# Raw loads of the first three head pairs over two hardware DMA queues, values first in the other queue, early relus on two engines, the last store in two

## The chip, the cores and the metric

The kernel runs on one core of a Trainium2 chip. The core has a matrix engine (TensorE; PE in the profile, its weight loads PEld), VectorE (DVE), ScalarE (ACT), GpSimd (POOL) and SyncE (SP), which here only issues DMAs. Data moves between device memory and the core's on-chip memory by DMA, on 16 DMA engines that all queues share. POOL feeds one queue (software_dynamic in the profile, q0), in which a transfer may also cast; SP and ScalarE feed hardware queues (hardware_dynamic, q1), which copy as is. The metric is the device time in microseconds (us).

## What is computed

Attention with one added to the softmax's denominator, and then a feed-forward layer with a squared relu:

```python
# q, k, v: (8 batches, 12 heads, 448 positions, 64), fp32
scores = scale * q @ k^T                      # scale = 1/8
e = exp(scores - m)                           # m: row maximum
attn = e / (sum(e) + exp(-m) + 1e-9)          # exp(-m) is the added one
x = (attn @ v).transpose(0, 2, 1, 3).reshape(3584, 768)
h = x @ w_in                                  # 768 -> 2048
g = relu(h) ** 2
out = g @ w_out                               # 2048 -> 768, fp32
```

The kernel takes no maximum: it computes `exp(scores)` and divides by `sum + 1`, which is the same.

## The kernel before

**Tiling.** Heads are taken in pairs, two heads of 64 on the 128 partitions, so that a batch has six pairs. A unit of attention is a pair of one batch: `scores` (q k^T into PSUM, L163), `exp` on ScalarE (L153), `add_chunks` on VectorE (sums over the key chunks, L194), `row_sums` (a matmul with ones, then logarithm and negated exponential on ScalarE, that is, a reciprocal, L225), `values` (L218) and `normalise` on VectorE into the tile `xt` (L237). Batch 0 has twelve units: six pairs with 192 queries each, then six with the other 256. The other batches have six units of 448 queries. The order is software-pipelined by hand (L372 to 416): in iteration i, the scores and exponentials of unit i stand with the row sums, values and normalisation of unit i - 1.

**Feed-forward.** `mlp_in` (L247) and `mlp_out` (L272) are generators. When a stretch of tokens is normalised, they are queued, and `drain` puts some of their matmuls between the steps of the attention units, by a share that is set where they are queued. The first stretch has 128 tokens. For it `mlp_in` takes four blocks of 128 hidden columns at a time (`f0` = 0, 4, 8, 12), each followed by a relu on ScalarE (L263) and a square on VectorE (L267). For all other stretches the relu is on VectorE (L265). `mlp_out` copies each block of 128 tokens from PSUM in two pieces of 512 and 256 columns (ScalarE, L283) and then stores the 768 columns in one go (SP, L295).

**Loads and queues.** Weights, values and most of q and k come by POOL's queue and are cast to fp16 on the way. For batches 0 and 1, q and k lie in the on-chip memory as they are read ("natural"); `regroup` on VectorE (L139) puts them in order, PE transposes them (L146), and VectorE copies the result from PSUM (L149). Regrouping stands two units ahead of the scores, transposing one. So the regroup of pair 3 stands on VectorE in iteration 1, ahead of that unit's `add_chunks`. For later batches, q and k go through a staging buffer and a transposing DMA.

In the order in which the loads are issued: q and k of pairs 0 and 1 of batch 0 as fp32 by SP (tiles `qr`, `kr`, L88); by POOL (tiles `qn`, `kn`, L91; `vn`, L79) q and k of pair 2, v of pairs 0 to 2, then, after the identity for the transposes has been made on POOL, q, k and v of pairs 3 to 5, four of eight parts of `win`, and then batch 1 and the rest of the weights. A tile `qn` or `kn` is used again by batch 1, whose load waits for the last regroup from it. Nine matmuls on zeros (L363) run on PE at the start, and more of them between the first units.

The instructions of an engine run in the order of the program. Each tile pool has a fixed number of buffers; the pool of the reciprocal has one for each of its two tiles.

Of the kernel before, what the change touches and what calls it, by code (L numbers as in the profile page):

```python
# [8 lines left out]
FP32 = mybir.dt.float32  # L9
FP16 = mybir.dt.float16  # L10
AF = mybir.ActivationFunctionType
# [4 lines left out]
def kernel(  # L16
# [9 lines left out]
    nc = tc.nc  # L26

    B, H, S, D = q.shape
    NT, DM = out.shape
# [4 lines left out]
    RUN = 4  # L34
    P = S // RUN
    ON_PE = (0, 1)
    COLS = H * S // 2 + 16

    scale = 1.0 / float(D) ** 0.5
# [11 lines left out]
    z_pool = ctx.enter_context(tc.tile_pool(name="z", bufs=1))  # L51
# [6 lines left out]
    m_psum = ctx.enter_context(tc.tile_pool(name="m_psum", bufs=3, space=bass.MemoryType.PSUM))  # L58

    ctx.enter_context(tc.manual_schedule())  # L60
    nc.scalar.preload_act_table_set("natural_log_exp_and_others")

    win = persist.tile([128, DCH, DF], FP16, name="win")
    wout = persist.tile([128, NFFB, DM], FP16, name="wout")
# [10 lines left out]
    def load_v(b, p0, p1):  # L75
        hs = slice(2 * p0, 2 * p1)
        if b not in vns:
            vns[b] = v_pool.tile([P, H, RUN, D], FP16, name="vn")
        nc.gpsimd.dma_start(out=vns[b][:, hs], in_=v_r[b, :, hs])  # L79

    def load_natural(b, p0, p1):

        raw = b == 0 and p1 <= 2
        for n, r in (("q", q_r), ("k", k_r)):
            src = r[b, :, 2 * p0:2 * p1]
            if raw:
                t = nat.tile([P, 2, RUN, D], FP32, name=f"{n}r{p0}")
                nc.sync.dma_start(out=t, in_=src)  # L88
            else:
                t = nat.tile([P, NPAIR, RUN, D], FP16, name=f"{n}n{p0 // 3}")  # L90
                nc.gpsimd.dma_start(out=t[:, 0:2 * (p1 - p0)], in_=src)  # L91
            for pr in range(p0, p1):
                naturals[n, b, pr] = t[:, 2 * (pr - p0):2 * (pr - p0) + 2]
# [115 lines left out]
    def of_head(e, u, h):  # L209

        b, _, _, n = u
        if n < S:
            return e[:, h]
        if b in ON_PE:
            return e.rearrange("p (h x) -> p h x", h=2)[:, h]
        return e.rearrange("p (o h x) -> p h o x", o=2, h=2)[:, h]
# [8 lines left out]
    def row_sums(u, es):  # L225
        n = u[3]
        total = es[:, 0:2 * S] if n == S else es[:, 4 * S - 2 * n:4 * S].rearrange("p (h n) -> p h n", h=2)
        zp = m_psum.tile([128, 512], FP32, name="mp")
        for h in range(2):
            nc.tensor.matmul(zp[64 * h:64 * h + 64, 0:n], ones, of_head(total, u, h), start=True, stop=True)  # L230
        lnz = z_pool.tile([128, S], FP32, name="lnz")
        rcp = z_pool.tile([128, S], FP32, name="rcp")
        nc.scalar.activation(out=lnz[:, 0:n], in_=zp[:, 0:n], func=AF.Ln, bias=one_b)  # L233
        nc.scalar.activation(out=rcp[:, 0:n], in_=lnz[:, 0:n], func=AF.Exp, scale=-1.0)  # L234
        return rcp

    def normalise(u, xp, rcp):  # L237
# [9 lines left out]
    def mlp_in(t0, n):  # L247
        gt = gts[t0] = []
        xt, x0 = xts[t0 // (2 * S)], t0 % (2 * S)
        per = max(1, 512 // n) if n < 384 else 1  # L250
        for f0 in range(0, NFFB, per):
            hp = m_psum.tile([128, 512], FP32, name="mp")
            for j in range(per):
                fb = f0 + j
                for dc in range(DCH):
                    nc.tensor.matmul(hp[:, j * n:(j + 1) * n], win[:, dc, fb * 128:(fb + 1) * 128],  # L256
                                     xt[:, dc, x0:x0 + n], start=(dc == 0), stop=(dc == DCH - 1))
                    if j < per - 1 or dc < DCH - 1:
                        yield n / 2.4
            m = per * n  # L260
            rt = r_pool.tile([128, 512], FP16, name="rt")
            if t0 == 0:
                nc.scalar.activation(out=rt[:, 0:m], in_=hp[:, 0:m], func=AF.Relu)  # L263
            else:
                nc.vector.tensor_scalar(out=rt[:, 0:m], in0=hp[:, 0:m], scalar1=0.0, scalar2=None, op0=ALU.max)  # L265
            g = g_pool.tile([128, 512], FP16, name=f"g{f0}")
            nc.vector.tensor_mul(g[:, 0:m], rt[:, 0:m], rt[:, 0:m])  # L267
            for j in range(per):
                gt.append(g[:, j * n:(j + 1) * n])
            yield n / 2.4  # L270

    def mlp_out(t0, n):  # L272
        gt = gts.pop(t0)
        for ts in range(n // 128):
            ot = osb_pool.tile([128, DM], FP32, name="ot")
            for n0, n1 in ((0, 512), (512, DM)):
                op = m_psum.tile([128, 512], FP32, name="mp")
                for fb in range(NFFB):
                    nc.tensor.matmul(op[:, 0:n1 - n0], gt[fb][:, ts * 128:(ts + 1) * 128], wout[:, fb, n0:n1],  # L279
                                     start=(fb == 0), stop=(fb == NFFB - 1))  # L280
                    if fb < NFFB - 1:
                        yield (n1 - n0) / 2.4
                nc.scalar.activation(out=ot[:, n0:n1], in_=op[:, 0:n1 - n0], func=AF.Copy, scale=OUT_SCALE)  # L283
                if n1 < DM:
                    yield (n1 - n0) / 2.4
            c = t0 + ts * 128
            end = c + 128
            while c < end:
                b = c // S
                step = RUN if b in ON_PE else 2  # L290
                rows = out[b * S:(b + 1) * S, :].rearrange("(p t) m -> t p m", t=step)
                t, p = c % S // (S // step), c % (S // step)
                m = min(S // step - p, end - c)
                o = c + 128 - end
                nc.sync.dma_start(out=rows[t, p:p + m, :], in_=ot[o:o + m, :])  # L295
                c += m
            yield (DM - 512) / 2.4


# [3 lines left out]
    nc.vector.memset(ones, 1.0 / GS)  # L303
    one_b = consts.tile([128, 1], FP32)
    nc.vector.memset(one_b, 1.0 / GS)
    load_natural(0, 0, 1)
    load_natural(0, 1, 2)
    load_natural(0, 2, 3)
    load_v(0, 0, 3)
    ident = consts.tile([128, 128], FP16)  # L310
    make_identity(nc, ident)
# [16 lines left out]
    def queue(part, t0, n):  # L328
        work.append((mlp_in if part == 1 else mlp_out)(t0, n))
        left[0] += (NFFB * DCH * n if part == 1 else n // 128 * NFFB * DM) / 2.4  # L330
# [17 lines left out]
    t0 = 384  # L348
    for b in range(1, B):
        n = 384 if b % 2 == 0 else 512  # L350
# [21 lines left out]
    for i in range(NU + 1):  # L372
# [6 lines left out]
        if u:  # L379
            b, pr = u[0:2]  # L380
# [16 lines left out]
        if prev:  # L397
            rcp = row_sums(prev, pes)
            values(prev, pet, xp, 0)
            values(prev, pet, xp, 1)  # L400
            if i < NPAIR:
                keep_warm(1)
# [44 lines left out]
```

The softmax here doesn't subtract the row's maximum and nothing guards it: scores larger than these inputs give would overflow.

## Time and profile before

| what | value |
|---|---|
| median of four runs | 437.62 us (435.66 to 438.82) |
| the profiled execution | 438.7 us, span 436.9 us |
| PE busy | 426.3 us, 98% of the span |
| ACT busy | 248.4 us, 57% |
| DVE busy | 244.8 us, 56% |
| POOL busy | 33.4 us, 8% |
| mean granted clock of PE | 0.992 |
| POOL's DMA queue | 24608 packets, 22.40 MB |
| hardware DMA queues | 54304 packets, 24.34 MB |

The span goes from the first to the last instruction of one execution; the time of that execution is 1.8 us longer. Busy shares are over the whole span and hide that the start and the end look different from the middle. A line of the profile names the engine, the line of the code, the operation and the tiles; "idle before, releaser" says how long the engine stood idle ahead of an instruction and what ended that. In the chain of work that ended last, each step is followed back to what released it.

### The profile page before, as it was taken

Reading aid. Unit: us, or ns where it says so; the run is one execution under the profiler, and the core shown is the slowest. Engines: PE = TensorE matmul, PEld = TensorE weight load, DVE = VectorE, ACT = ScalarE, POOL = GpSimd, SP = SyncE. Lnnn points to the kernel's source line nnn. Section 1 sums busy time; section 2 is a strip of 40 time slices with the busy share of each in tenths; the row PEclk is TensorE's granted clock in tenths of the full one; section 3 lists DMA queues with packets and bytes.
Section 4 is the critical chain, followed back from the end, with each engine's and each line's share of the span. In section 5 each row is a group of like instructions: output and inputs, shape, how many; then the busy total and the mean of one; then the engine's idle time right before and its main releaser. Section 6 shows DMA issues by size and latency. Waiting matters only on the chain.

```text
span 436.9 us, 7530 instructions
## 1 busy us (share of the span) xinstructions
PE 426.3 (98%) x3147; PEld 231.5 (53%) x3147; DVE 244.8 (56%) x487; ACT 248.4 (57%) x361; POOL 33.4 (8%) x52
## 2 busy tenths in 40 slices
PE   8989899999999999999999999999999999999996
PEld 3556574544455555554456555654455555554464
DVE  3857585358822586348842388248762278428700
ACT  2889767664565756675446755764555655740011
POOL 8441100010000100010000100030000000000000
PEclk9989899999999999999999999999999999999999
DMA  9999999289312894259611698039902200010022
GB/s 173 197 197 203 210 213 191 74 145 194 78 38 75 136 204 77 66 83 214 128 27 54 101 224 123 38 56 208 190 1 74 72 3 1 36 59 14 1 72 72
DMA packets 78946, 47.22 MB, mean 108 GB/s; under 512 B 50624, under 2 KB 74944, under 8 KB 78528
## 3 DMA queue, kind: packets, MB, share of 16 engines
q0 software_dynamic: 24608, 22.40, 32.3%
q1 hardware_dynamic: 54304, 24.34, 24.8%
q8 instruction: 24, 0.39, 0.3%
q14 instruction: 10, 0.08, 0.1%
HBM read 45.71 MB, written 19.32 MB: 149 GB/s over the span
## 4 chain that ended last, share of the span: by engine, by line
PE 92%; ACT 3%; DMA 2%; issue 1%; POOL 1%; DVE 1%; ACTq 0%; POOLq 0%
PE mp L256 34%; PE mp L279 34%; PE sp L186 9%; PE xp L222 8%; PE mp L230 3%; PE sp L174 2%; DMA kn<-in_k_dram 2%; ACT et L154 1%; PE mp L146 1%; ACT lnz L233 1%; ACT rcp L234 0%; POOL qn L91 0%; DVE es L203 0%; POOL vn L79 0%; PE mp L363 0%
## 5 line engine op out<-in xcount | busy, mean ns | idle before, releaser
L154 ACT ACTIVATE et<-sp 112x896 f16<-112x896 f32 (+2 forms) x192 | 166.2, 914 | 115.8 <-PE sp L186 94.2
L256 PE MATMUL mp<-xt,win 128*128 128x512 f16 (+3 forms) x864 | 156.9, 335 | 1.5 <-DVE xt L242 1.5
L279 PE MATMUL mp<-wout,g 128*128 128x512 f16 (+1 forms) x896 | 154.2, 326 | 0.0
L279 PEld LDWEIGHTS <-g 128*128 128x128 f16 x896 | 84.2, 98 | 63.2 <-issue 9.6
L256 PEld LDWEIGHTS <-win 128*128 128x128 f16 x864 | 78.4, 99 | 72.2 <-issue 12.6
L199 DVE TENSOR_TENSOR es<-et 112x896 f16<-112x896 f16 x84 | 51.6, 622 | 104.9 <-ACT et L154 104.8
L265 DVE TENSOR_SCALAR rt<-mp 128x512 f16<-128x512 f32 (+1 forms) x120 | 76.0, 633 | 38.5 <-PE mp L256 35.8
L283 ACT ACTIVATE ot<-mp 128x512 f32<-128x512 f32 (+1 forms) x56 | 27.3, 487 | 64.5 <-PE mp L279 63.7
L267 DVE TENSOR_TENSOR g<-rt 128x512 f16<-128x512 f16 (+1 forms) x124 | 49.5, 399 | 6.9 <-ACT rt L263 2.7
L222 PE MATMUL xp<-et,vn 112*64 112x448 f16 (+2 forms) x432 | 46.0, 335 | 0.0
L186 PE MATMUL sp<-qk 64*112 64x224 f16 x576 | 42.8, 268 | 0.0
L186 PEld LDWEIGHTS <-qk 64*112 64x112 f16 x576 | 26.9, 128 | 25.8 <-issue 25.8
L233 ACT ACTIVATE lnz<-mp,one_b 128x448 f32<-128x448 f32 (+2 forms) x54 | 32.2, 597 | 2.0 <-PE mp L230 1.9
L242 DVE TENSOR_TENSOR xt<-xp,rcp 128x448 f16<-128x448 f32 (+2 forms) x54 | 30.5, 566 | 2.7 <-ACT rcp L234 2.7
L234 ACT ACTIVATE rcp<-lnz 128x448 f32<-128x448 f32 (+2 forms) x54 | 28.9, 535 | 1.7
L222 PEld LDWEIGHTS <-vn 112*64 112x64 f16 x432 | 24.5, 110 | 10.0 <-issue 0.4
L79 POOL DMA_DIRECT2D vn<-in_v_dram x10 | 8.9, 890 | 246.8 <-PE xp L222 233.3
L201 DVE TENSOR_TENSOR es<-es 112x896 f16<-112x896 f16 x42 | 26.2, 623 | 1.0
L230 PE MATMUL mp<-es,ones 112*64 112x448 f16 (+2 forms) x108 | 19.4, 355 | 1.8 <-DVE es L207 1.6
L174 PE MATMUL sp<-qk 64*112 64x192 f16 (+2 forms) x144 | 17.3, 315 | 1.5 <-ACT et L154 1.3
L363 PE MATMUL mp<-warm 128*128 128x512 f16 x31 | 11.6, 479 | 1.2 <-DVE warm L301 1.2
L230 PEld LDWEIGHTS <-ones 112*64 112x64 f16 x108 | 6.4, 106 | 11.2 <-issue 5.0
(32 smaller groups left out, 83.2 us busy)
## 6 DMA issues: line engine op xcount, KB each, us to landing
out_dram<-ot SPq DMA_DIRECT2D x12, 384.0 KB, 2.3
vn<-in_v_dram POOLq DMA_DIRECT2D x6, 672.0 KB, 8.8
stage_q<-in_q_dram POOLq DMA_DIRECT2D x5, 676.0 KB, 11.2
stage_k<-in_k_dram POOLq DMA_DIRECT2D x5, 676.0 KB, 13.8
win<-in_moe_w_in_dram POOLq DMA_DIRECT2D x8, 384.0 KB, 14.7
wout<-in_moe_w_out_dram POOLq DMA_DIRECT2D x4, 768.0 KB, 19.5
out_dram<-ot SPq DMA_DIRECT2D x8, 288.0 KB, 2.6
out_dram<-ot SPq DMA_DIRECT2D x8, 192.0 KB, 2.7
```

The lines of the kernel that those rows point to most:

```text
L154: nc.scalar.activation(out=out_, in_=in_, func=AF.Exp, scale=scale)
L186: nc.tensor.matmul(sp[:, odd, h * (S // 2):(h + 1) * (S // 2)], qk[r, which, kx:kx + 2 * P - 1:2], qk[r, 0, x:x + S // 2], start=True, sto ...
L199: nc.vector.tensor_add(f[:, step], e[:, 2 * step], e[:, 2 * step + 1])
L222: nc.tensor.matmul(xp[64 * h:64 * h + 64, 0:n], vns[b][:, 2 * pr + h, kk, :], of_head(chunk(et, u, c, kk), u, h), start=(kk == 0), stop=(k ...
L230: nc.tensor.matmul(zp[64 * h:64 * h + 64, 0:n], ones, of_head(total, u, h), start=True, stop=True)
L233: nc.scalar.activation(out=lnz[:, 0:n], in_=zp[:, 0:n], func=AF.Ln, bias=one_b)
L234: nc.scalar.activation(out=rcp[:, 0:n], in_=lnz[:, 0:n], func=AF.Exp, scale=-1.0)
L242: nc.vector.tensor_mul(xts[b // 2][:, pr, c:c + n], xp[:, 0:n], rcp[:, 0:n])
L256: nc.tensor.matmul(hp[:, j * n:(j + 1) * n], win[:, dc, fb * 128:(fb + 1) * 128], xt[:, dc, x0:x0 + n], start=(dc == 0), stop=(dc == DCH - 1))
L265: nc.vector.tensor_scalar(out=rt[:, 0:m], in0=hp[:, 0:m], scalar1=0.0, scalar2=None, op0=ALU.max)
L267: nc.vector.tensor_mul(g[:, 0:m], rt[:, 0:m], rt[:, 0:m])
L279: nc.tensor.matmul(op[:, 0:n1 - n0], gt[fb][:, ts * 128:(ts + 1) * 128], wout[:, fb, n0:n1], start=(fb == 0), stop=(fb == NFFB - 1))
```

## The change

Five edits, all in one step:

1. q and k of pair 2 of batch 0 are loaded as fp32 into tiles of their own, like pairs 0 and 1. The q loads of the three pairs are issued by SP, the k loads by ScalarE, whose preload of the function table now stands behind them.
2. POOL's queue so begins with v of pairs 0 to 2.
3. Of the four relus of the first stretch, those of `f0` = 4 and 12 go to VectorE.
4. The logarithm is written to the tile of the reciprocal, and the tile `lnz` is gone.
5. Storing is a function of its own. For the last 128 tokens the first 512 columns are stored as soon as they are copied, and the other 256 after that.

```diff
-    nc.scalar.preload_act_table_set("natural_log_exp_and_others")
...
-        raw = b == 0 and p1 <= 2
+        raw = b == 0 and p1 <= 3
...
-                nc.sync.dma_start(out=t, in_=src)
+                (nc.sync if n == "q" else nc.scalar).dma_start(out=t, in_=src)
...
-        lnz = z_pool.tile([128, S], FP32, name="lnz")
         rcp = z_pool.tile([128, S], FP32, name="rcp")
-        nc.scalar.activation(out=lnz[:, 0:n], in_=zp[:, 0:n], func=AF.Ln, bias=one_b)
-        nc.scalar.activation(out=rcp[:, 0:n], in_=lnz[:, 0:n], func=AF.Exp, scale=-1.0)
+        nc.scalar.activation(out=rcp[:, 0:n], in_=zp[:, 0:n], func=AF.Ln, bias=one_b)
+        nc.scalar.activation(out=rcp[:, 0:n], in_=rcp[:, 0:n], func=AF.Exp, scale=-1.0)
...
-            if t0 == 0:
+            if t0 == 0 and f0 % 8 == 0:
                 nc.scalar.activation(out=rt[:, 0:m], in_=hp[:, 0:m], func=AF.Relu)
...
+    def store(c, ot, n0, n1):
+        end = c + 128
+        while c < end:
+            b = c // S
+            step = RUN if b in ON_PE else 2
+            rows = out[b * S:(b + 1) * S, n0:n1].rearrange("(p t) m -> t p m", t=step)
+            t, p = c % S // (S // step), c % (S // step)
+            m = min(S // step - p, end - c)
+            o = c + 128 - end
+            nc.sync.dma_start(out=rows[t, p:p + m, :], in_=ot[o:o + m, n0:n1])
+            c += m
...
                 nc.scalar.activation(out=ot[:, n0:n1], in_=op[:, 0:n1 - n0], func=AF.Copy, scale=OUT_SCALE)
+                if n1 == DM or t0 + ts * 128 + 128 == NT:
+                    store(t0 + ts * 128, ot, 0 if n1 < DM or t0 + ts * 128 + 128 < NT else n0, n1)
...
-    load_natural(0, 0, 1)
-    load_natural(0, 1, 2)
-    load_natural(0, 2, 3)
+    for pr in range(3):
+        load_natural(0, pr, pr + 1)
+    nc.scalar.preload_act_table_set("natural_log_exp_and_others")
     load_v(0, 0, 3)
```

More of the change, by code (lines that the diff above doesn't have):

```diff
@@ L283, in mlp_out @@
                 nc.scalar.activation(out=ot[:, n0:n1], in_=op[:, 0:n1 - n0], func=AF.Copy, scale=OUT_SCALE)
+                if n1 == DM or t0 + ts * 128 + 128 == NT:
+                    store(t0 + ts * 128, ot, 0 if n1 < DM or t0 + ts * 128 + 128 < NT else n0, n1)
                 if n1 < DM:
                     yield (n1 - n0) / 2.4
[L286 to L296, printed above, removed]
             yield (DM - 512) / 2.4
```

## The prediction

> **What bounds the kernel now.** I read the page first: its span, the granted clock by slices, the shares of the chain that ended last. Columns of the clock row are 40 equal slices in tenths.
>
> ```profile
> span 436.9 us, 7530 instructions
> ...
> PEclk9989899999999999999999999999999999999999
> ...
> PE 92%; ACT 3%; DMA 2%; issue 1%; POOL 1%; DVE 1%; ACTq 0%; POOLq 0%
> ```
>
> The matrix engine is 92% of the chain and is busy 426.3 us of 436.9. What is not matrix work lies in the first 50 us, before the feed-forward backlog fills every gap, and in the last 4 us. No edit takes a matmul away, so only those two stretches can give or cost anything. The clock row has two 8s there (slices 3 and 5, each 10.9 us). Next I read the chain in order of time (start, length, what), up to 50 us.
>
> ```profile
> 5.11 8.85 DMA kn<-in_k_dram
> 13.96 0.02 issue
> 13.98 0.30 DVE flatk L139
> ...
> 36.95 0.49 ACT rt L263
> 37.45 0.02 issue
> 37.47 0.43 DVE g L267
> ```
>
> The start hangs on one load: k of pairs 3 to 5 of batch 0, the fifth DMA in POOL's queue. VectorE stood 1.08 us before L139 for it, with the exponential sums of unit 1 behind it in order, and everything to 25 us follows. Later an early relu on ScalarE sits on the chain. The timeline shows the second such relu between two pairs of exponentials, and the issue of the last store:
>
> ```profile
> 45.73 0.60 ACT L263 ACTIVATE rt<-mp 128x512 f16<-128x512 f32 x1
> 46.21 1.74 ACT L154 ACTIVATE et<-sp 112x896 f16<-112x896 f32 x2
> ...
> 433.29 0.35 SPq L295 DMA_DIRECT2D out_dram<-ot  x1
> ```
>
> Then the busy time by stretches of 3.4 us (columns: length, PE, PEld, DVE, ACT, POOL busy, granted clock, DMA share, GB/s):
>
> ```profile
> 24.10:27.50 3.40, 1.93 (x26) 1.20 (x27) 1.88 (x5) 2.77 (x5) 1.60 (x3) 1.00 1.45 197
> 27.50:31.00 3.50, 3.50 (x32) 2.52 (x33) 1.45 (x3) 2.28 (x4) 1.45 (x2) 0.51 1.46 200
> ...
> 44.60:48.00 3.40, 2.07 (x22) 1.14 (x18) 2.25 (x8) 3.40 (x6) 0.23 (x1) 1.00 1.16 210
> 48.00:51.40 3.40, 3.40 (x20) 2.41 (x20) 2.11 (x4) 2.34 (x4) 1.75 (x3) 0.50 1.16 210
> ```
>
> Twice a stretch with little matrix work is followed by one at half clock. A stretch with 2.48 us of matrix work (37.80 to 41.20) was not. Each slow stretch costs up to 3.4 x 0.5 = 1.7 us.
>
> Last, packets in three windows of the DMA view: 2.5 to 3 us (hardware queue alone), 4.5 to 6 (both queues, 279 of the 448 from the hardware one), 10 to 14 (POOL's queue alone):
>
> ```profile
> DMA packets 180, 0.17 MB, mean 342 GB/s; under 512 B 13, under 2 KB 180, under 8 KB 180
> DMA packets 448, 0.35 MB, mean 231 GB/s; under 512 B 31, under 2 KB 448, under 8 KB 448
> DMA packets 1570, 0.78 MB, mean 196 GB/s; under 512 B 40, under 2 KB 1570, under 8 KB 1570
> ```
>
> That is 360, 299 and 393 packets per us. A packet carries 256 numbers in either queue (1,024 bytes raw, 512 after the cast), so the raw form costs about the same time; what costs is the mixing of the two.
>
> **The change, part by part.**
>
> *Loads.* Pair 2's q and k (2 x 240 packets; four raw loads made 960) leave POOL's queue and go raw; k of all three pairs goes by ScalarE's queue, v is first in POOL's. The packets ahead of the load that gates at 13.96 stay the same in number. Two effects decide.
> Gain: two queues fill the engines earlier; the windows 1.5:2 and 2:2.5 held 34 and 117 packets against 180 at full rate, and if the second window fills and a part of the first, about 100 packets come early, 100/393 = -0.25 us.
> Loss: the mixture lasts longer. The hardware queue moved 279/1.5 = 186 packets per us in it, so 480 more take 2.6 us, each us of which moves 94 fewer packets than POOL's queue alone: 243 packets, +0.6 us.
> I take +0.35 us on the landing, so 14.3 instead of 13.96.
> Bounds: from 3.25 to 8 us 1387 packets passed where 393 per us would be 1867. If that loss went, the load would land 1.2 us sooner; only the 1.08 us of the wait can be gained, so -1.1. If bytes and not packets count, the 0.23 MB more take 1.2 us at 196 GB/s: +1.2. I take the value between, because the three rows above are of this very stage.
>
> One rule weighs against this part. The Trainium skill's page "DMA: Bandwidth & Descriptors", section "Issuing engines are not separate DMA queues", says that DMAs of all issuers interleave on the same 16 engines, so that a second issuer saves only issue time. By that rule the sum for this part would be about 0 instead of +0.35.
>
> *What the moved steps pass.* POOL issues two DMAs fewer (0.82 + 0.67 us), so v is issued at 1.30 instead of 2.78 and the identity is ready near 2.9 instead of 4.40. The first transposes do not gain: they stand behind nine warm-up matmuls that end at 5.2. ScalarE issues three DMAs before its table load: 3 x 0.47 (SP's longest) + 1.28 ends near 3.5; its first exponential is at 7.57, so 4 us cover it. Pairs 0 and 1 may land sooner, but the wait for the gating load swallows that. Pair 2 must be there at 10.4, when VectorE is free; at the mixed rate the hardware queues are through at 3 + (1440 - 331)/186 = 9.0, and 0.3 later landed, so no wait. Its regroup reads fp32: 0.43 and 0.55 to 0.71 us instead of 0.28 and 0.29, +0.4 to 0.6 us on VectorE, covered by its idle 0.34 and 1.08 us; if the load came early, this would be late next. The next q and k loads of batch 1 lose their wait for pair 2's buffer (1.07 us of POOL at 11.02); the engines are full anyhow: 0.
>
> *Relus.* There are four for the first 128 tokens; those of f0 = 4 and 12 move to VectorE, where one takes 0.69 us (the row at 51.85, same shape) instead of 0.58 to 0.60.
> First, at 36.86: VectorE is idle from 35.55, the eleven matmuls that end the group finish at 36.46, so relu to 37.2 and square to 37.6 instead of 37.9: -0.3. Bounds: +0.1 (it starts when ScalarE's did) to -0.49 (all of it on the chain).
> Second, at 45.73: ScalarE is busy 3.40 of 3.40 there, the exponentials move up by 46.21 - 45.73 = 0.48. VectorE does the relu from 45.87 to 46.56, the sums behind it at 46.71 slip by 0.2 and the next sum has 0.65 of idle before it: -0.48. Bounds -0.2 to -0.6.
> Together -0.8 (-1.1 to -0.1).
>
> *One tile less for the reciprocal.* The logarithm now writes the tile that the last normalise reads, so it waits for VectorE; behind it stand the next unit's exponentials, for which PE waits. Normalise ends ahead of the next logarithm by 0.57 us at 15.4, by 3.7 us in the steady part (101.63 against 105.36), at the least by 0.12 (39.29 against 39.41). Cost 0, bounds 0 to +0.2.
>
> *Last store.* The last 384 KB were moved from 434.08 to 435.18. The first two thirds now go from 431.8, behind the last matmuls. The rest is a third: 0.37 instead of 1.10 us, -0.73. Against that, 384 KB and 96 KB stores land in median 2.3 and 2.2 us, -0.1. I take -0.6, nearer the tail's own row.
>
> **Sum:** 0.35 - 0.8 - 0.6 = -1.05 us. The profiled execution took 438.7 (span 436.9 and 1.8 around it), so 437.65. It stands 1.1 above the median 437.62 of the runs, so the median becomes 436.6. From no change this kernel can be told by about 0.5%, 2.2 us: the likeliest outcome is a gain too small to tell.
>
> **Rivals.**
>
> *A slow stretch goes.* The stretch 44.60 to 48.00 had 2.07 us of matrix work; 0.48 us less waiting puts 2.55 in it, over the 2.48 that passed. Then 48.00 to 51.40 runs at full clock: 436.6 - 1.7 = 434.9. Against: the places of such stretches may differ from run to run (the four runs differ by 3.2 us), so the median may hold it only in part. The skill's page "TensorE: Matmul & The Clock Gate", Part 1, says that the gate judges free-running windows of about 3.4 us; by it a slow stretch hits only runs whose window falls over the gap, and the sum of -1.05 would hold in the runs that it misses either way.
>
> *The loads land early.* The mixing loss goes: -1.1 instead of +0.35, 435.1. The 299 row speaks against it.
>
> *Slower.* The gating load lands late and the clock falls. Place: 13.9 to 17.3, where PE had 2.97 us of work. If the load comes 0.9 us late or more, that falls to 2.07 and the next 3.4 us run at half clock. Price: 1.2 - 0.35 + 1.7 = +2.55 on the sum, 439.1; without the clock, 437.4. For it: in the mixture the byte rate was 231 GB/s, not 342. Against it: a packet carries as many numbers in either queue.
>
> *It does not do what it says.* If VectorE's relus come too late and the tail's store lands by its receipt alone, -0.1 and -0.1 remain with +0.35: 437.8.
>
> **How the numbers follow.** Likeliest (436.6) 0.45, its own range 435.6 to 437.6; slow stretch gone 0.25 (434.9); loads early 0.07 (435.1); nothing gained 0.12 (437.8); slower 0.11 (439.1, or more with a second slow stretch). Faster by over 0.5% (under 435.4) holds most of the second and third case: 0.29. Slower by over 0.5% (over 439.8) takes about half of the last and some of the fourth for the runs' own spread: 0.09. Same: 0.62. The range reaches from below the slow-stretch case, 434.2, to the slower case's lower part, 438.8.
>
> **What would show it.** Right: VectorE's wait before flatk of pair 3 ends at 14 to 14.6 with the same loads in front; relus on VectorE near 36.5 and 45.9, with exponentials of ScalarE back to back around the latter; the last packets end about 0.6 us after the last store's first. Wrong: the gating load before 13.5 or after 14.9; a clock row with one 8 or three; a logarithm that waits for normalise.

## The result

The changed kernel takes 435.84 us in the median (44 runs, 435.13 to 437.5), the kernel before 437.3 us (69 runs, 435.55 to 442.24). The ratio is 0.9969, with a 95% interval of 0.996 to 0.9978: 1.4 us faster, 0.3%. The forecast was 1.05 us, 436.6 us, in a range of 434.2 to 438.8. The sum came out near; of its three terms the relus were too small, the loads had the wrong sign, and the store was right in itself but did not show. One run of the kernel with one hardware queue, at 443.06 us, counts as slow and is left out of its median and ratio below.

The page of the changed kernel's profiled execution (435.75 us; span, granted clock by slices, chain by engine):

```profile
span 433.9 us, 7478 instructions
...
PEclk9989999999999999999999999999999999999999
...
PE 88%; DMA 7%; POOL 1%; DVE 1%; ACT 1%; issue 1%; POOLq 0%
```

One 8 is left in the clock row where there were two, and DMA has gone from 2% of the chain to 7%. The two profiled spans differ by 3.0 us, twice the difference of the medians: the execution shown of before was one with two slow stretches. The chain in order of time (start, length, what) says where the DMA share lies:

```profile
7.68 16.23 DMA win<-in_moe_w_in_dram
...
24.48 14.47 DMA kn<-in_k_dram
...
38.97 0.29 DVE flatk L138
```

The chain no longer passes through k of batch 0's pairs 3 to 5. It goes through POOL's queue as a whole, down to k of pairs 3 to 5 of *batch 1*, issued behind the last input weights. VectorE's timeline (start, length, operation, idle before and what ended it):

```profile
13.33 0.30 DVE L138 COPY flatk<-kn 112x512 f16<-112x512 f16 x1 [0.37 <-DMA kn<-in_k_dram]
27.48 0.29 DVE L138 COPY flatk<-kn 112x512 f16<-112x512 f16 x1 [1.20 <-DMA kn<-in_k_dram]
35.30 0.69 DVE L263 TENSOR_SCALAR rt<-mp 128x512 f16<-128x512 f32 x1 [0.37 <-PE mp L254]
38.97 0.29 DVE L138 COPY flatk<-kn 112x512 f16<-112x512 f16 x1 [0.39 <-DMA kn<-in_k_dram]
```

The first line is the wait that gated the start: the copy begins at 13.33 instead of 13.98. The second and fourth are where the compute has caught up with the loads; the second wait was 0.24 us before, the fourth was not there. The third is the first relu on VectorE. Busy time in the stretches shown of before (length, PE, PEld, DVE, ACT, POOL, clock, DMA share, GB/s):

```profile
24.10:27.50 3.40, 1.93 (x24) 1.24 (x22) 1.60 (x5) 2.67 (x5) 1.53 (x2) 0.87 1.45 197
27.50:31.00 3.50, 3.50 (x39) 2.47 (x37) 2.16 (x5) 2.20 (x5) 1.51 (x2) 0.64 1.45 198
44.60:48.00 3.40, 2.97 (x32) 1.91 (x31) 3.30 (x7) 3.37 (x6) 1.71 (x3) 1.00 1.16 210
48.00:51.40 3.40, 3.40 (x32) 2.11 (x31) 1.32 (x3) 2.17 (x4) 0.27 (x1) 1.00 1.16 210
```

The first slow stretch (3.4 us at half clock, here from 26.6 us) is still there. Between 44.6 and 48.0 PE now does 2.97 us of work instead of 2.07, and what follows runs at full clock.

VectorE's copies of the transposed q and k (the PSUM copy in each unit) make a yardstick along the start. They stand 0.66 us earlier than before from 14.7 to 19 us, 1.44 earlier at 37.8 (after the first moved relu), 1.31 at 40.8 (the load at 38.97 took some back), 1.9 at 47.6; the last copy to the output starts 3.17 us earlier (429.71 against 432.88), the second slow stretch being gone.

### The profile page after: what moved, and what is told of

Same layout as the page of the kernel before. It is cut to its first block, busy times and chain, and to the rows that moved or that the text cites. A ratio compares the mean times of both kernels' runs of the same rounds, so it can differ in the third digit from the quotient of the medians.

```text
span 433.9 us, 7478 instructions
## 1 busy us (share of the span) xinstructions
PE 424.5 (98%) x3147; PEld 230.2 (53%) x3147; DVE 246.4 (57%) x489; ACT 246.7 (57%) x359; POOL 32.0 (7%) x50
## 4 chain that ended last, share of the span: by engine, by line
PE 88%; DMA 7%; POOL 1%; DVE 1%; ACT 1%; issue 1%; POOLq 0%
PE mp L289 35%; PE mp L254 33%; PE sp L185 9%; PE xp L221 7%; DMA win<-in_moe_w_in_dram 4%; DMA kn<-in_k_dram 3%; PE mp L229 3%; PE sp L173 1%; POOL win L96 1%; ACT et L153 1%; POOL vn L78 0%; DVE xt L240 0%; POOL kn L90 0%; POOL qn L90 0%; DVE es L198 0%
## 5 line engine op out<-in xcount | busy, mean ns | idle before, releaser
L263 DVE TENSOR_SCALAR rt<-mp 128x512 f16<-128x512 f32 (+1 forms) x122 | 77.4, 634 | 37.7 <-PE mp L254 35.1
L231 ACT ACTIVATE rcp<-mp,one_b 128x448 f32<-128x448 f32 (+2 forms) x54 | 32.2, 596 | 1.8 <-PE mp L229 1.8
L232 ACT ACTIVATE rcp<-rcp 128x448 f32<-128x448 f32 (+2 forms) x54 | 28.9, 535 | 1.7
```

Source lines behind the costliest of these rows:

```text
L231: nc.scalar.activation(out=rcp[:, 0:n], in_=zp[:, 0:n], func=AF.Ln, bias=one_b)
L232: nc.scalar.activation(out=rcp[:, 0:n], in_=rcp[:, 0:n], func=AF.Exp, scale=-1.0)
```

## The experiments

Each run has a mean granted clock besides its time. One stretch of 3.4 us at half clock lowers the mean over 437 us by 3.4 x 0.5 / 437 = 0.004, so about 0.996 means one such stretch, about 0.992 two. (The clock can also fall behind the last matmul: in the changed kernel's profile it is half from 432.8 us on. That moves single values by up to 0.003.) The 95 runs of the kernel before that stood beside the twelve experiments sort as follows: clock 0.9975 or more, 35 runs, median 436.35 us; about 0.996, 28 runs, 437.35; about 0.992, 28 runs, 438.63; lower, 4 runs, 439.5. The changed kernel's 44 runs: 11 runs, 435.57; 30 runs, 435.85; 3 runs, 436.99. Some runs were on other chips, so 0.3 us between such groups says little; but before, a slow stretch costs about 1 us each, and in the changed kernel the first one costs 0.3 and a second is rare (3 of 44 against 32 of 95). The changed kernel is also shorter in every group, by 0.8 us without a slow stretch, 1.5 with one and 1.6 with two. So the gain has three parts, which the numbers of runs put at about 0.8 us in runs without a slow stretch, 0.4 from the lower price of the first stretch and 0.4 from the rarer second one.

**The kernel before, once more.** No edit.

> The kernel before, run once more for its pairs of time and mean granted clock. Two theories on the 1.4 us between the medians. Sum: the parts shorten the chain in every run (0.65 us at the gating load, about 1.3 at the two relus); then the fastest runs of before stay 1.3 us or more above the fastest of the changed kernel. Clock: the changed kernel mostly loses the second half-clock stretch (48 to 51 us); then the times of before go with the mean clock, runs with a clock of 0.996 or more lie within 0.5 us of the changed kernel's 435.6, and those at 0.992 some 2 to 3 us above.

Median 437.4 us, ratio 0.999 (0.9966 to 1.0014). Five runs at clock 1.0 took 435.43 to 436.58, four at 0.996 took 437.28 to 437.68, three below that 438.14 to 439.71. The fastest runs of before reach the changed kernel's median, so the sum theory, which kept them 1.3 us above its fastest, fails. The times go with the clock, as the clock theory says, but it fails at 0.996: those runs lie 1.7 to 2.1 us above 435.6, where it allowed 0.5. Neither theory alone gives the 1.4 us.

**Loads alone** (with the one tile that makes room for them).

```diff
-        raw = b == 0 and p1 <= 2
+        raw = b == 0 and p1 <= 3
...
-                nc.sync.dma_start(out=t, in_=src)
+                (nc.sync if n == "q" else nc.scalar).dma_start(out=t, in_=src)
...
-        lnz = z_pool.tile([128, S], FP32, name="lnz")
```

> Before, with the loads of pairs 0 to 2 as in the changed kernel and the reciprocal in one tile; all four early relus on ScalarE, last store whole. Sum: flatk of pair 3 at 13.3 instead of 13.98, and the median 0.6 us below before. Floor: k of batch 1's pairs 3 to 5 lands near 39 us in either kernel, so what is gained before it can be swallowed there; then the median moves by 0.3 us or less and VectorE shows a longer wait for that load. My prediction's own step (landing 0.35 us later, by mixing of the queues) would make it 0.3 us slower.

Median 436.92 us, ratio 0.9989 (0.9962 to 1.0015): no difference that this can tell. The copy of k of pair 3 starts at 13.23 without any wait, so in this execution the load does land about 0.7 us earlier, and not 0.35 later as my sum had it. In the median nothing of it is seen. Sorted by clock, against all runs of before on the same chip, there is something: 435.86 against 436.33 us without a slow stretch, 436.92 against 437.58 with one, 438.15 against 438.68 with two, four runs of this kernel in each group.

**Relus alone.**

```diff
-            if t0 == 0:
+            if t0 == 0 and f0 % 8 == 0:
```

> Before, with the relus of f0 = 4 and 12 on VectorE and nothing else. Sum: the iteration around 34.5 to 39.2 us shortens by 0.8 us and the one around 44.9 to 49.5 by 0.5, median 1.3 us below before. Floor: flatk of batch 1's pair 3 then waits for its load at 38.7, which takes part of the 0.8 back; median 0.7 to 1.0 us below. Clock: the stretch 44.6 to 48.0 holds over 2.5 us of matrix work and the half-clock stretch behind it is gone in most runs; the median is then 1.2 us or more below and the spread of the runs half of that of before.

Median 435.74 us (435.44 to 436.6), ratio 0.9962 (0.9946 to 0.9979): this one line alone gives as much as the whole change. No run has more than about one slow stretch (lowest clock 0.994), where 19 of the 47 runs of before on the same chip have two or more. The runs are also shorter at the same clock: 435.53 against 436.33 us without a slow stretch, 436.31 against 437.58 with one. VectorE waits 1.15 us for k of batch 1 at 38.98. The stretch that decides, and the one behind it:

```profile
44.60:48.00 3.40, 2.97 (x32) 1.95 (x31) 3.27 (x7) 3.37 (x6) 1.70 (x3) 1.00 1.16 210
48.00:51.40 3.40, 3.40 (x32) 2.11 (x31) 1.28 (x3) 2.17 (x4) 0.27 (x1) 1.00 1.16 210
```

**The changed kernel with its relus back on ScalarE.**

```diff
-            if t0 == 0 and f0 % 8 == 0:
+            if t0 == 0:
```

> The changed kernel with all four early relus on ScalarE again. Sum: 1.3 us above the changed kernel. Clock: the half-clock stretch at 48 us is back in many runs, the median 0.8 to 1.5 us above the changed kernel and the spread as wide as that of before; the fastest runs as fast as those of the changed kernel. Loads and store alone carry the gain only if it stays within 0.3 us of the changed kernel.

Median 437.35 us, 435.49 to 438.45, ratio to before 0.9984 (0.9963 to 1.0005). Six of twelve runs are back at clock 0.992, and the fastest three (435.49 to 435.92) are as fast as the changed kernel. Its profiled execution is instructive:

```profile
44.60:48.00 3.40, 2.08 (x22) 1.14 (x19) 2.25 (x7) 3.40 (x6) 0.31 (x1) 1.00 1.16 210
```

The same 2.08 us of work as in the execution before, and here the clock does not fall afterwards (1.00 from 48.00 to 51.40). The rows above are cut at fixed times; the slow stretches of the profiles are not. Each lasts 3.41 us. In the execution before they begin at 27.54 and 48.02 us, 20.48 apart, which is six times 3.41. In this execution there is one in the start, from 27.03, so the fifth stretch of 3.41 us after it begins at 44.10. First the second slow stretch of before, then these two here:

```profile
48.02:51.43 3.41, 3.41 (x21) 2.41 (x21) 2.09 (x4) 2.32 (x4) 1.73 (x3) 0.50 1.16 210
...
27.03:30.44 3.41, 3.41 (x31) 2.34 (x29) 1.74 (x4) 1.80 (x3) 1.51 (x2) 0.50 1.45 197
...
44.10:47.51 3.41, 2.50 (x27) 1.55 (x26) 2.66 (x8) 3.41 (x6) 0.00 (x0) 1.00 1.16 210
```

Cut in this way, the stretch that counts held 2.50 us of work, and before, from 44.61 to 48.02, 2.08. In the fourteen profiles all eight slow stretches between 20 and 60 us follow 3.41 us with 1.68 to 2.14 us of matrix work. None follows 2.20 or more, and two stretches with 1.94 and 1.95 (relus alone, before once more) were not followed by one, so the work alone does not decide. The start of this grid of 3.41 us moves from execution to execution (the first slow stretch begins between 26.60 and 28.13 us). That agrees with the free-running window that the Trainium skill's page "TensorE: Matmul & The Clock Gate", Part 1, describes.

**Batch 1's q and k moved forward in POOL's queue.**

```diff
-    for i in range(4):
+    for i in range(2):
         load_win(i, 8)
     load_natural(1, 0, 3)
-    for i in range(4, 8):
+    for i in range(2, 6):
         load_win(i, 8)
     load_natural(1, 3, 6)
+    for i in range(6, 8):
+        load_win(i, 8)
```

> The changed kernel with batch 1's q and k loads moved forward in POOL's queue: pairs 0 to 2 behind the second part of the input weights instead of the fourth, pairs 3 to 5 behind the sixth instead of the eighth. Same bytes. Floor theory: VectorE's waits for k of batch 1 (1.20 us at 27.5, 0.39 at 39.0) go, the rows of regroup move up by 0.4 to 1.2 us, and the fastest runs fall from 435.1 to 434.0 to 434.8; the median falls by about as much if the slow clock does not come back. If the loads do not set the floor, nothing changes beyond 0.2 us. Weights for the third and fourth block of the first tokens land at about 36 and 38 us and could be late for PE at 37 to 41: then the gain is lost in a wait of PE for the input weights.

Median 435.56 us, ratio 0.997 (0.9951 to 0.9988), no better than the changed kernel's 0.9969. But its four runs at clock 0.9975 or more took 434.42 to 434.69, below every run of the changed kernel (lowest 435.13), six at about 0.995 took 435.42 to 436.33, and two at 0.992 and 0.991 took 436.8 and 438.33. VectorE in that kernel:

```profile
26.03 0.27 DVE L138 COPY flatk<-kn 112x512 f16<-112x512 f16 x1
...
36.97 0.28 DVE L138 COPY flatk<-kn 112x512 f16<-112x512 f16 x1
```

No wait is left before either copy of k (a wait would stand behind the line in brackets), and the second stands 2.0 us earlier than in the changed kernel. So the order of the loads did set a floor, the shortest time of the runs without a slow stretch; and with the floor gone, the first slow stretch costs about 1 us again (435.67 against 434.56).

**The same with six matmuls on zeros ahead of the first feed-forward matmuls.**

```diff
-            if i < NPAIR:
-                keep_warm(1)
+            if i < NPAIR or i == NPAIR + 1:
+                keep_warm(1 if i < NPAIR else 6)
             drain(share * 0.45)
```

> As the one with the loads moved forward, and six matmuls on zeros on PE in iteration 7, ahead of the first feed-forward matmuls that wait for the last normalise (24.9 to 26.8 us). Clock theory: matmul work of 24.1 to 27.5 rises from 1.93 to about 3.2 us, the half-clock stretch from 27.5 to 31 goes in nearly all runs, and the median falls by 0.5 to 1.5 us against the one without them, provided that the wait for the loads no longer swallows it. Otherwise six matmuls at 0.216 us in an idle gap cost 0 to 0.3 us.

Median 434.89 us, ratio 0.9946 (0.9925 to 0.9967), lowest clock 0.997. Work in 24.1 to 27.5 was 2.98 us, and no half-clock stretch followed.

**The six matmuls without moving the loads.** The edit just shown, on the changed kernel.

> The changed kernel with the six matmuls on zeros in iteration 7 alone, the loads of batch 1 where they were. Floor theory: the half-clock stretch from 27.5 to 31 goes, but the wait for k of batch 1 near 39 us swallows it, as runs of the changed kernel at clock 1.0 and 0.994 both take 435.6: median 435.6 to 436.0, within 0.2 of the changed kernel's fast majority. If the clock alone set the time, the median falls to 434.9, as with the loads moved forward.

Median 435.92 us, ratio 0.9971 (0.9953 to 0.9989): as the changed kernel. In the profiled execution the work in 24.1 to 27.5 rose to 3.23 us and the clock stayed whole behind it, for nothing. The wait for the loads and the slow stretch cover each other: taking away either alone gives nothing in the median, taking away both gives about 0.25% by the ratios, whose intervals just overlap.

**One hardware queue instead of two.**

```diff
-                (nc.sync if n == "q" else nc.scalar).dma_start(out=t, in_=src)
+                nc.sync.dma_start(out=t, in_=src)
```

> The changed kernel with q and k of pairs 0 to 2 all issued by SP. In the changed kernel POOL's queue moves its first packet at 6.5 us, in the kernel before at 3.1. If the second hardware queue crowds it out, its first packets come near 3 to 4 us here, and the gating load lands as in my prediction's mixture, 14.0 us or later. If its own longer first load (v, 672 packets instead of 224) is the cause, the first packet still comes at about 6.5. Median within 0.3 us of the changed kernel in either case, since the relus carry the gain.

Median 437.42 us (eleven runs), ratio 1.0018 (0.9992 to 1.0044): 0.5% above the changed kernel's ratio, so my "within 0.3 us" was wrong, and the copy that waits for the gating load begins at 15.06. Packets from 3 to 4 and from 5 to 6 us with one queue (q0 is POOL's, q1 SP's):

```profile
q1 hardware_dynamic: 252, 0.24, 97.6%
q0 software_dynamic: 15, 0.01, 7.8%
...
q1 hardware_dynamic: 35, 0.03, 19.5%
q0 software_dynamic: 263, 0.13, 101.2%
```

and in the changed kernel from 3 to 4 and from 6 to 7 us (q10 is ScalarE's):

```profile
q10 hardware_dynamic: 211, 0.20, 58.6%
q1 hardware_dynamic: 179, 0.17, 49.7%
...
q1 hardware_dynamic: 125, 0.12, 57.0%
q10 hardware_dynamic: 104, 0.11, 47.4%
q0 software_dynamic: 24, 0.01, 8.9%
```

With one hardware queue, POOL's packets begin in the fourth microsecond and at times push the raw loads aside (35 against 263). With two, none of POOL's moves before the seventh (in one of the other six profiles with two queues a couple of packets came at 5.8 us), though its first load is the same and is issued at the same 1.31 us. So its longer first load does not hold POOL's queue back; the raw loads on two queues do. That SP alone also issues the last raw load later, at 3.2 us where the two had all six issued by 2.2, was not separated from the number of queues.

**The changed kernel with its last store whole.**

```diff
-                if n1 == DM or t0 + ts * 128 + 128 == NT:
-                    store(t0 + ts * 128, ot, 0 if n1 < DM or t0 + ts * 128 + 128 < NT else n0, n1)
+                if n1 == DM:
+                    store(t0 + ts * 128, ot, 0, n1)
```

> The changed kernel with the last 128 tokens stored in one go again. My prediction: 0.6 us slower from the end of the last copy to the end of the span (bounds 0.1 and 0.73). From the profiles so far: 4.0 us from the start of the last copy to the end in the kernel before, 4.2 in the changed one, where an instruction load lies among the last packets. If that load is what took the gain back, the end takes 4.4 here, as with the loads alone; without it 4.0.

Median 436.38 us, 0.5 above the changed kernel; the ratio is 0.9981 (0.9965 to 0.9997), and the intervals of the two overlap. From the last copy's start (429.07) to the end (434.5) it takes 5.4 us, more than I had put for either case. SP's wait for the last store in this kernel, and the instruction packets from 430 us on:

```profile
SPq L443 <- DMA out_dram<-ot: 2.8, 1, 2.8
```

```profile
q14 instruction: 2, 0.02, 0.9%
```

**Two stores alone.** The two edits of the store, on the kernel before.

> Before, with the last 128 tokens stored in two pieces and nothing else. My prediction's step: 0.6 us less from the start of the last copy to the end of the span, 3.4 instead of 4.02 us, SP's wait for the last store 1.0 to 1.2 instead of 1.8, and no instruction load among the last packets, as in the kernel before. Median 0.6 us below before, which the spread of before may hide. If the two-piece store itself is worth nothing, the end stays at 4.0.

Median 436.64 us, ratio 0.9987 (0.9966 to 1.0007). The median does not resolve it, though sorted by clock the runs lie below before on the same chip in each group, by 0.9, 0.5 and 0.8 us. The end does: the last copy starts at 433.20, the span ends at 436.6, 3.40 us instead of 4.02. The term of 0.6 us was right. SP's wait, of before first, of this kernel second:

```profile
SPq L442 <- DMA out_dram<-ot: 1.8, 1, 1.8
```

```profile
SPq L445 <- DMA out_dram<-ot: 1.1, 1, 1.1
```

**One tile alone.** The three edits of `lnz` and `rcp`, on the kernel before.

> Before, with logarithm and reciprocal in one tile and nothing else. It has 52 instructions fewer on ScalarE's side (one wait instead of two). My prediction: cost 0 to 0.2 us. Theory from the profiles so far: this edit, and not the loads, moves an instruction load into the last microseconds and lengthens the close after the last store, so the end takes 4.4 to 5.4 us instead of 4.02 and the median is 0.4 to 1.0 above before at the same clock. If the end stays at 4.0, it was the loads.

Median 436.59 us, ratio 0.9989 (0.9974 to 1.0005). The end takes 4.17 us instead of 4.02, and no instruction load lies there (one comes 0.3 us after the span has ended), so the theory that this edit alone brings one into the end is refuted. An instruction load is a transfer in the profile's queue row "instruction". In the profiles, one stood in the last 6 us of the span of every kernel with the raw loads of pair 2 (among the packets of the last store in five of them, just before or after it in three) and of none without them. The same eight kernels share a second loss: after the store SP waits 1.2 us for PE's queue, against 0.7 in the five kernels with neither edit and 0.8 here. With those loads the two reciprocal tiles do not fit into on-chip memory, so the loads were not tried without the one tile; whether it needs both edits is open.

**What the runs point to:** relus, two stores, loads of batch 1 moved forward and six matmuls on zeros, on the kernel before, without the raw loads and without the one tile.

```diff
-            if t0 == 0:
+            if t0 == 0 and f0 % 8 == 0:
...
+                if n1 == DM or t0 + ts * 128 + 128 == NT:
+                    store(t0 + ts * 128, ot, 0 if n1 < DM or t0 + ts * 128 + 128 < NT else n0, n1)
...
-    for i in range(4):
+    for i in range(2):
         load_win(i, 8)
...
+                keep_warm(1 if i < NPAIR else 6)
...
```

> Before, with the shared relus, the store in two, batch 1's q and k moved forward in POOL's queue and six matmuls on zeros in iteration 7; the first loads and the two tiles of the reciprocal as before. If loads and one tile are worth nothing or cost time at the end, this is at or below the changed kernel with the same two additions (434.9): median 434.0 to 434.9, end 3.4 us. If the raw loads on two queues are worth their 0.3 to 0.6 us, it lies at 435.2 or above.

Median 434.17 us (433.76 to 434.35, all six at clock 0.9975 or more), ratio 0.9929 (0.9908 to 0.9949). It beats both kernels, and lies 0.7 us below the version that also has the raw loads and the one tile (434.89, on another chip; the ratios are 0.9929 and 0.9946, and their intervals overlap). The end takes 3.39 us here and 4.30 there, which is enough to cover the difference. The stretch of the first slow clock:

```profile
24.10:27.50 3.40, 3.23 (x36) 1.79 (x32) 1.79 (x5) 2.76 (x6) 1.30 (x2) 1.00 1.45 197
27.50:31.00 3.50, 3.38 (x55) 2.58 (x49) 2.58 (x7) 3.47 (x6) 1.50 (x2) 1.00 1.45 199
```

## Why the prediction was right or wrong

**Direction and size, right:** -1.36 us by the ratio against -1.05. That the size is so near is partly luck: the relus alone give what the whole change gives, and the other two terms, +0.35 and -0.6, both show in profiles and neither in a median. Of the signs that I had named for being wrong, two came true: the gating load landed before 13.5, and one 8 is left in the clock row.

**What bounds the start, half right.** The load at 13.96 did gate. But I let every microsecond gained there run through to the end. It meets two things on the way: the loads of batch 1 in the same queue, whose waits (0.24 us before, 1.20 and 0.39 in the changed kernel) stand in no term of my sum, and the slow stretches.

**Loads, wrong in sign:** +0.35 predicted, -0.65 in the profiled pair. Packets up to 8 us and up to the landing of the gating load (13.96 and 13.30 us), of before first and then of the changed kernel:

```profile
DMA packets 1795, 1.33 MB, mean 166 GB/s; under 512 B 92, under 2 KB 1795, under 8 KB 1795
DMA packets 4106, 2.48 MB, mean 178 GB/s; under 512 B 150, under 2 KB 4106, under 8 KB 4106
...
DMA packets 1685, 1.50 MB, mean 188 GB/s; under 512 B 93, under 2 KB 1685, under 8 KB 1685
DMA packets 3771, 2.55 MB, mean 191 GB/s; under 512 B 144, under 2 KB 3771, under 8 KB 3771
```

The step on the mixture came out near, though not in the way that I had worked it out: by 8 us 110 packets fewer had passed, which at 393 per us is 0.28 us late. POOL's queue begins at 6.7 us instead of 3.1, and the raw loads on two queues take its place. The gain that I gave for filling earlier did not come: from 2 to 3 us 107 packets moved, 297 before. The failed step is the sentence that the packets ahead of the gating load stay the same in number. When it landed, 335 fewer had passed, which is 0.85 us at that rate: fewer packets of the loads that stand behind it in POOL's queue went first. This is not the same in every execution. Four of the seven profiles with two queues had 3757 to 3791 packets by then and the load at 12.9 to 13.3 us; the other three had 4024 to 4151, and it landed at 13.78, 13.96 and 14.55. In the six profiles with the loads of before it landed between 13.78 and 14.30. The means are 13.5 and 14.0. What decides between the two cases stays open. The case "loads early" had the right landing for the profiled pair (its bound was -1.1) and the wrong price, since the loads alone are worth nothing that the medians can tell. The rule of the skill's page "DMA: Bandwidth & Descriptors" on issuing engines, by which a second issuer saves only issue time, put this part at about 0. For the order in which the queues are served the runs show more than it says: on one hardware queue or two, the copy behind the gating load begins at 15.06 or 13.33.

**Relus, right in mechanism, too small:** -0.8 predicted (bounds -1.1 to -0.1), -1.32 in the two iterations. The first iteration went from 4.68 to 3.85 us, -0.83 instead of -0.3. The part that failed is where the group of matmuls ends: I took all eleven from 35.67 as its own and had the relu wait for the last of them. In the changed kernel VectorE's relu starts 0.3 us after the eleven begin (35.30 against 34.98), long before they end at 35.77, so the first few of them end the group. The second iteration went from 4.67 to 4.18, -0.49 as predicted.

**Slow stretch goes:** I gave this rival 0.25, as a further case. It is a part of the gain, not an alternative to the sum: a second slow stretch is in 3 of 44 runs instead of 32 of 95, and the runs without any are shorter as well. The work was read rightly: 2.97 us where 2.55 was expected, above the 2.48 that passed. The place does drift from run to run, as the rival's caveat said: the execution with the relus back on ScalarE had the same 2.08 us in the same row, but 2.50 in the stretch that counted, and stayed at full clock.

**One tile, cost 0:** the waits of the logarithm for normalise cost nothing that shows; the bound of +0.2 holds the 0.15 us at the end of its own run.

**Last store, right alone, hidden in sum:** 0.6 us predicted, 0.62 measured alone. In the changed kernel the end takes 4.19 us, no less than the 4.02 of before. Against two stores alone (3.40), SP waits 0.4 us longer for the last store, among whose packets an instruction load lies, and 0.5 longer for PE's queue after it. I priced neither. Without the split the end takes 5.4.

**Slower:** the gating load came earlier, not later, so this rival's point (0.9 us late) was not reached. With one hardware queue it was (15.06), and that kernel lost against the changed one, though not clearly against before. But it did not lose in the place that I named: from 13.90 to 17.30 its profile has 3.15 us of matrix work, not 2.07, and full clock behind it; the slow stretch there begins at 28.0.

## What to carry to other kernels

A gain early in a start-up is worth what is left after the next two waits, so look for the next load in the same queue before pricing the first. Where the clock falls after an idle stretch, sort the runs by their mean clock first: a small edit that moves work into the idle stretch can move the median by more than the time it saves, and two such causes can cover each other, so that each has to be taken away together with the other. An edit that is worth 0.6 us at the end can be hidden by what other edits put there; read the last 5 us of the changed kernel's own DMA view and of SP's waits.

## What the runs showed of the hardware that I had not expected

With two hardware queues loaded, POOL's queue moved its first packet at 6.7 us, although its DMA was issued at 1.31 us; with one hardware queue, at 3 to 4 us. The first packets of the two queues themselves came more slowly: 102 to 213 packets from 2 to 3 us in the kernels with two queues, 266 to 298 in those with one.

With an instruction load (about 0.01 MB) among its packets, the last store has stragglers: where it was whole, all but 7 of its 144 packets had gone by 431.5 us, and single ones went on to about 432.4. SP waited 2.8 us instead of 1.8. Where the instruction load came before or after the store's packets, SP waited 1.0 us for a store in two pieces, against 1.5 to 1.8 with it among them. That the load holds one engine's share back is argued from these packets, not shown.

One stretch of 3.4 us at half clock goes with 1.0 to 1.3 us in the runs of the kernel before, not the 1.7 that half of 3.4 us gives, and with 0.3 us in the changed kernel, where a wait for a load follows behind it.
